# A fused attention and feed-forward kernel: ScalarE's function table loaded by a small exponential at the start, and another list that sets the order of all work

## The chip, the cores and the metric

The kernel runs on one core of one Trainium2 chip. The time is device microseconds of one execution. Three executions of the kernel before took 293.28 to 294.3 us, median 293.74.

## The reference

Sliding-window attention with a linear bias by distance, over 8 batches, 8 heads, 576 positions and a head size of 64, and then a feed-forward layer with a squared relu; in short:

```python
scores = scale * np.matmul(q, k.transpose(0, 1, 3, 2))
rel = pos[:, None] - pos[None, :]
bias = slopes[:, None, None] * (-np.abs(rel).astype(np.float32))[None, :, :]
mask = (rel >= 0) & (rel < window)                 # window = 128
scores = np.where(mask, scores + bias[None], -1000000000.0)
attn = softmax(scores)
x = np.matmul(attn, v)                             # to 4608 tokens of 512
h = x @ w_in                                       # 512 -> 2048
g = np.maximum(h, 0.0) ** 2
out = g @ w_out                                    # 2048 -> 512
```

Inputs and output are float32; the kernel computes in bfloat16 with float32 accumulation.

## The kernel before

The positions are cut into blocks of up to 128, numbered m = 0 to 35. The first block of each of the 8 batches (0 to 7) has no block before it; blocks 8 and up see the block before them too. For each block the work is: load q and k (`lkq`) and v (`lv`), transpose q and k (by TensorE with copies out, `tp` and `ev`, for blocks 0 to 7; by DMA transposes on SyncE's queue, `kqT`, after that), scores (`s`), exponentials on ScalarE (`e`), masks on VectorE (`m`), the product with v (`pv`), its normalisation on VectorE (`r`, `n`), and a transpose of the result (`xp` and `x`; `x` alone, by DMA, from block 8 on). Blocks 0 to 3 take their bias into PSUM by two matmuls of `ident` with `slopes` (`b`, line 774) ahead of the scores; the others are multiplied by `masks`, exponentials of the distance.

Block 0 is special: SyncE and ScalarE issue the loads of its k and q as float32 (`lk0`, `lq0`, line 523), VectorE casts them (`ck0`, `cq0`), and TensorE transposes k (`tp0.0`, line 610) and q (`tp0.1`). All other loads stand in GpSimd's queue: q and k, v, the weights w_in in five pieces (`w_in`), w_out in four (`w_out`). A first load waits in the queue behind nothing but GpSimd's own work, such as the `iota` that gives the distances; `ident` and `dist` (lines 423, 429, 430) are made from it by VectorE, and `slopes` from `dist` by VectorE and ScalarE.

Tokens are worked in 9 groups g of 512. The up phase (512 -> 2048) of groups 0 to 2 is direct (`u`, units of 8 or 16 matmuls); groups 3 to 8 use Strassen-like products with sums of weights (`us`) and of tokens (`ut`): `f`, in seven products, with sums and copies on VectorE and ScalarE. Relu and square (`relu`, `sq`) follow on ScalarE or VectorE. The down phase (2048 -> 512) is direct for group 0 (`o`, quarters of an output tile) and Strassen-like for the rest (`p`, seven products of two halves, `S1` to `S4` sums of g on VectorE, `ws` weight differences).

What sets the order: a list of about 1,680 task names, `ORDER`, written out in the kernel. Each name's instructions are emitted in that order; a trailing `+` picks the second of a task's possible engines, `:n` its PSUM banks. Every engine executes its own instructions in the emitted order, with semaphore waits between engines. The planner's durations (`BEGIN`, `S_PE`, the numbers in `plan.add`) pick nothing any more, except one thing: where the plan sees a gap ahead of a TensorE task in the first 30 us, `fill` (line 376) emits stand-in matmuls of zeros into that task's bank, one for each 56 ns of 0.85 of the gap. Eight larger stand-ins run at the very start (`warm`, line 574).

Of the kernel before, what the change touches and what calls it, by code (L numbers as in the profile page):

```python
# [36 lines left out]
S_PE = 360.0  # L37
# [16 lines left out]
    lk0.0 lk0.1 lkq1 warm0 one0.1 warm:6 one0.0 lq0.0 lq0.1 iota lkq2 ident dist1 slope0.3+ slope0.1+ slope1.0  # L54
    slope1.2 slope1.1 slope1.3+ slope0.2 ck0 lv0 slope0.0 b0:36 tp0.0:2 ev0.0.2 lv1 ev0.0.0+ cq0 w_in0 one0.7 one0.3
    one0.4 lv2 tp0.1:2 ev0.1.0 ev0.1.2 tp1.0:4 tp1.1:7 ev1.0.0+ w_in1 ev1.0.2+ s0 ev1.1.2+ ev1.1.0 e0.0 b1:50 e0.1
    one0.2 one0.5 one0.6 tp2.0:7 lkq3 tp2.1:1 s1 ev2.0.2+ ev2.0.0 ev2.1.2+ ev2.1.0 e1.0 pv0.0:6 pv0.1:3 r0.0 b2:17
    r0.1 n0.0 w_in4 s2 e1.1 n0.1 pv1.0:4 lv3 e2.0 pv1.1:5 r1.0 b3:36 n1.0 e2.1 xp0.0:2 r1.1 lkq4 n1.1 x0.0 pv2.0:0
    pv2.1:1 r2.0 xp1.0:7 n2.0 u0.0.0:2 x1.0 r2.1 n2.1 reluu0.0.0 lkq5 mask1.4 xp2.0:5 mask1.0 squ0.0.0 u0.1.0:4 x2.0
    tp3.0:0 mask1.2 reluu0.1.0 u0.0.1:1 w_in2 ev3.0.0+ ev3.0.2 tp3.1:7 u0.3.0:0 reluu0.0.1 ev3.1.2 w_in3 ev3.1.0  # L60
    squ0.0.1+ s3 squ0.1.0 lv4 reluu0.3.0 dist0 e3.0 u0.2.5:2 e3.1 w_out0 pv3.0:1 r3.0 pv3.1:5 u0.2.4:6 r3.1
    reluu0.2.5 one1.2 tp4.0:7 one1.0 one1.1 n3.0 n3.1 reluu0.2.4 one1.7 one1.6 tp4.1:3 xp3.0:4 ev4.1.0 tp5.0:5 x3.0+
    tp5.1:2 u0.5.2:4 lv5 lkq6 ev5.0.0+ squ0.2.4 w_out1 u0.5.3:6 ev5.1.0 one1.5 mask1.3 squ0.3.0 ev4.0.0+ squ0.2.5+
# [20 lines left out]
    r11.0 s13 n11.0 x10 pv11.1:3 u2.0.0:0 e13.0 r11.1 n11.1 e13.1 u2.0.2:4 e13.2 e13.3 x11 m12.0 m12.1 u2.0.6:1
    reluu2.0.2 m13.0 u2.0.4:6 us3.3 reluu2.0.0 st1.2.1 squ2.0.0 u2.0.1:4 kqT16 reluu2.0.4 u2.0.5:3 squ2.0.2 st1.3.1
    m13.1 pv12.0:0 pv12.1:5 lkq18 reluu2.0.5 st1.3.0 u2.0.7:7 squ2.0.4 reluu2.0.6 st1.7.3 st1.7.2 r12.0 squ2.0.5
    reluu2.0.1 u2.0.3:2 n12.0 reluu2.0.7 lv16 r12.1 kqT17 n12.1 squ2.0.6 squ2.0.7+ squ2.0.1 pv13.0:3 lv15 pv13.1:1
    reluu2.0.3 r13.0 s14 n13.0 st1.4.2 lv17 r13.1 u2.1.2:0 n13.1 e14.0 squ2.0.3 x12 lv18 e14.1 u2.1.0:4 mc14
# [5 lines left out]
    p2.5.1 lv21 n15.0 r15.1 n15.1 m16.1 x15 s17 s2_2 p2.7.0 p2.7.1 e17.0 S4.2.0 e17.2 c11_2 e17.1 lkq20 s5_2+ p2.3.0
    c22_2 kqT19 kqT21 e17.3 pv16.0:0 r16.0 m17.1 s18 n16.0 p2.3.1 m17.0 e18.0 e18.2 c12_2 e18.3 p2.4.0 kqT23
    pv16.1:4 m18.1 e18.1 r16.1 m18.0 pv17.0:5 pv17.1:0 n16.1 st2.2.0 st2.3.0 p2.4.1 s3_2 pv18.0:6 f3.0.1:7 f3.1.1:4
    r17.0 n17.0 st2.7.2 r17.1 s1.3.0:3 f3.2.1:5 n17.1 st2.2.1 ut3.0 ut3.1 s1.3.1:1 r18.0 lkq22 s1.3.2+:2 f3.0.2 x16
    pv18.1:0 reluf3.0.2 f3.0.6 s2.3.0 f3.1.2 n18.0 f3.0.5 sqf3.0.2 lv22 reluf3.1.2 ut3.2 ut3.3 f3.3.1:6 r18.1 s5.3.0
    f3.0.7 n18.1 kqT20 lv20 sqf3.1.2+ f3.2.2 c22.3.0 f3.0.3 c12.3.0 f3.1.6 reluf3.2.2 sqf3.2.2+ lkq25 x18 f3.1.5
    s2.3.1 f3.2.6 f3.0.4 reluc12.3.0 sqc12.3.0 f3.1.7 lkq26 s1.3.3+:3 s5.3.1 f3.1.3 st2.3.1 reluc22.3.0 sqc22.3.0+  # L100
    kqT22 reluf3.0.4 f3.3.2 reluf3.3.2 f3.2.5 c22.3.1 f3.1.4 c12.3.1 f3.3.6 s5.3.2 s2.3.2+ f3.2.7 sqf3.3.2+
    reluc22.3.1 sqf3.0.4 sqc22.3.1+ reluc12.3.1 f3.2.3 c22.3.2 c12.3.2 f3.3.5 p3.1.0:0 s2.3.3 st2.7.3 s5.3.3 x17
    f3.3.7 reluc22.3.2 reluc12.3.2 sqc12.3.2+ sqc22.3.2 sqc12.3.1 c22.3.3 reluc22.3.3 reluf3.1.4 f3.2.4 reluf3.2.4
# [5 lines left out]
    m22.1 p3.4.1 r21.0 s3_3 m22.0 pv21.1:5 kqT24 f4.0.1:7 s1.4.0:0 st3.7.3 f4.1.1:4 ut4.0 s1.4.1:3 n20.1 kqT26 n21.0
    ut4.1 pv22.0:2 lkq27 pv22.1:6 r22.1 f4.0.2 ut4.2 reluf4.0.2 f4.0.6 r22.0 n22.0 f4.1.2 ut4.3 n22.1 s2.4.0 r21.1  # L110
    f4.0.5 n21.1 s5.4.0 f4.0.7 lv23 f4.2.1:2 sqf4.0.2 lv24 f4.0.3 f4.1.6 reluf4.1.2 f4.1.5 sqf4.1.2+ c22.4.0 c12.4.0
    reluc12.4.0 s5.4.1+ s2.4.1 lv26 f4.0.4 reluc22.4.0 f4.1.7 s1.4.2:0 f4.2.2 reluf4.0.4 f4.1.3 sqc22.4.0+ sqc12.4.0
# [168 lines left out]
def kernel(  # L281
# [1175 lines left out]
```

## Time and profile before

| | |
|---|---|
| median of three executions | 293.74 us (293.28 to 294.3) |
| profiled execution, its own time | 294.23 us |
| span of the profiled execution, first to last instruction | 292.4 us |
| mean granted TensorE clock | 0.992 |
| busy: TensorE, VectorE, ScalarE, GpSimd | 281.1, 234.3, 207.3, 104.1 us |
| DMA packets, bytes | 159915, 39.68 MB |

The views used are: the page (busy time and share of each engine); the waits (engine and line that waited, what it waited for, us in total, times, longest); the stretches (busy time of each engine between two times, granted TensorE clock as a share of full speed, DMA share, GB/s); the timeline (start, length, engine, line, operation, output <- inputs, count, and in brackets the idle time before it and what ended it); the chain of waits that ended last (start, length, what); and a line's own view, which gives how long its DMAs took from issue to landing. PE is TensorE, PEld its weight loads, DVE is VectorE, ACT ScalarE, POOL GpSimd, SP SyncE; SPq and ACTq are DMA issues there. A matmul of 256 columns shows as 273 ns, since matmuls overlap; eight of them that follow each other advance 0.87 us.

### The profile page before, as it was taken

Reading aid. Unit: us, or ns where it says so; the run is one execution under the profiler, and the core shown is the slowest. Engines: PE = TensorE matmul, PEld = TensorE weight load, DVE = VectorE, ACT = ScalarE, POOL = GpSimd, SP = SyncE. Lnnn points to the kernel's source line nnn. Section 1 sums busy time; section 2 is a strip of 40 time slices with the busy share of each in tenths; the row PEclk is TensorE's granted clock in tenths of the full one; section 3 lists DMA queues with packets and bytes.
Section 4 is the critical chain, followed back from the end, with each engine's and each line's share of the span. In section 5 each row is a group of like instructions: output and inputs, shape, how many; then the busy total and the mean of one; then the engine's idle time right before and its main releaser. Section 6 shows DMA issues by size and latency. Waiting matters only on the chain.

```text
span 292.4 us, 9410 instructions
## 1 busy us (share of the span) xinstructions
PE 281.1 (96%) x3832; PEld 235.8 (81%) x3837; DVE 234.3 (80%) x570; ACT 207.3 (71%) x429; POOL 104.1 (36%) x132
## 2 busy tenths in 40 slices
PE   6799999999999999999899998999999999999994
PEld 2588745888889888887688887888888889888884
DVE  2545375968978698999799989999999998898933
ACT  3598933987847955887559964898868777777830
POOL 8965552709704744362427049550000000000000
PEclk9799999999999999999999999999999999999999
DMA  8999999999999999999999999999944112210123
GB/s 143 165 196 199 201 180 134 139 161 179 155 157 163 188 143 131 135 185 164 160 137 193 207 117 150 158 183 135 169 93 110 36 38 65 67 36 5 60 84 108
DMA packets 159915, 39.68 MB, mean 136 GB/s; under 512 B 142336, under 2 KB 159360, under 8 KB 159872
## 3 DMA queue, kind: packets, MB, share of 16 engines
q0 software_dynamic: 104432, 18.10, 86.7%
q1 hardware_dynamic: 54640, 20.33, 44.0%
q10 hardware_dynamic: 800, 0.66, 0.8%
q8 instruction: 30, 0.49, 0.7%
q14 instruction: 13, 0.11, 0.2%
HBM read 36.70 MB, written 9.44 MB: 158 GB/s over the span
## 4 chain that ended last, share of the span: by engine, by line
PE 86%; DVE 9%; ACT 2%; issue 1%; POOL 1%; DVEq 0%; POOLq 0%; ACTq 0%
PE o L1249 28%; PE h L1079 23%; PE h L977 15%; PE pv L830 6%; PE o L1160 5%; PE s L680 4%; DVE P L728 2%; PE tp L607 2%; DVE g L1384 1%; DVE rt L1104 1%; DVE sums L1384 1%; PE xp L874 1%; DVE g L948 1%; PE s L774 1%; PE o L1341 1%
## 5 line engine op out<-in xcount | busy, mean ns | idle before, releaser
L1249 PEld LDWEIGHTS <-g 128*128 128x128 bf16 x624 | 59.5, 98 | 9.2 <-issue 1.1
L1249 PE MATMUL o<-w_out_sb,g 128*128 128x256 bf16 x512 | 63.0, 273 | 1.4 <-DVE g L1384 0.9
L933 ACT ACTIVATE rt<-h 128x512 bf16<-128x512 f32 (+1 forms) x97 | 55.9, 596 | 11.3 <-PE h L1079 5.6
L545 POOL DMA_DIRECT2D kq<-in_k_dram x32 | 27.2, 855 | 69.5 <-DMA kqT<-kq 67.2
L715 ACT ACTIVATE E<-s 128x384 bf16<-128x384 f32 x96 | 41.3, 498 | 10.7 <-PE s L680 10.5
L977 PE MATMUL h<-xT,w_in_sb 128*128 128x256 bf16 (+1 forms) x432 | 44.8, 261 | 0.0
L948 DVE TENSOR_TENSOR g<-rt 128x512 bf16<-128x512 bf16 (+1 forms) x90 | 35.6, 415 | 9.5 <-ACT rt L933 8.9
L977 PEld LDWEIGHTS <-w_in_sb 128*128 128x128 bf16 x432 | 37.7, 98 | 4.2
L1079 PE MATMUL h<-xT,w_in_sb 128*128 128x256 bf16 x288 | 40.2, 273 | 0.2 <-DVE vf L400 0.2
L1079 PEld LDWEIGHTS <-w_in_sb 128*128 128x128 bf16 x384 | 36.4, 98 | 4.9 <-issue 0.4
L946 ACT ACTIVATE g<-rt 128x512 bf16<-128x512 bf16 (+1 forms) x55 | 34.2, 631 | 1.3 <-DVE rt L1112 0.7
L728 DVE TENSOR_TENSOR P<-E,masks 128x1024 bf16<-128x1024 bf16 x48 | 32.1, 679 | 3.3 <-ACT E L715 2.9
L402 ACT ACTIVATE osb<-o 128x512 f32<-128x512 f32 x30 | 18.0, 599 | 22.9 <-PE o L1249 19.0
L1249 PE MATMUL o<-wsum,sums 128*128 128x256 bf16 x256 | 30.6, 273 | 0.1
L854 DVE TENSOR_TENSOR x<-pv,rec 128x256 bf16<-128x256 f32 x72 | 29.1, 417 | 1.1
L551 POOL DMA_DIRECT2D vt<-in_v_dram x32 | 27.0, 865 | 8.1 <-PE pv L830 3.4
L545 POOL DMA_DIRECT2D kq<-in_q_dram x32 | 27.3, 854 | 6.6 <-DMA w_out_sb<-in_moe_w_out_dram 2.6
L1079 PE MATMUL h<-ut,kqf 128*128 128x256 bf16 x192 | 27.5, 273 | 0.0
L1249 PEld LDWEIGHTS <-sums 128*128 128x128 bf16 x256 | 24.3, 98 | 3.6 <-DVE sums L1384 0.4
L830 PEld LDWEIGHTS <-P 128*128 128x128 bf16 x512 | 21.9, 98 | 3.3 <-DVE P L728 1.1
L1104 DVE TENSOR_TENSOR rt<-h,vf 128x512 bf16<-128x512 f32 x32 | 21.7, 682 | 2.1 <-ACT vf L402 0.9
L830 PE MATMUL pv<-vt,P 128*128 128x65 bf16 x384 | 20.5, 193 | 0.1
(100 smaller groups left out, 432.2 us busy)
## 6 DMA issues: line engine op xcount, KB each, us to landing
out_dram<-osb SPq DMA_DIRECT2D x53, 128.0 KB, 4.0
kq<-in_k_dram POOLq DMA_DIRECT2D x31, 128.0 KB, 6.6
kq<-in_q_dram POOLq DMA_DIRECT2D x31, 128.0 KB, 7.3
vt<-in_v_dram POOLq DMA_DIRECT2D x24, 128.0 KB, 6.8
w_out_sb<-in_moe_w_out_dram POOLq DMA_DIRECT2D x4, 512.0 KB, 12.7
w_in_sb<-in_moe_w_in_dram POOLq DMA_DIRECT2D x3, 512.0 KB, 9.8
vf<-in_v_dram POOLq DMA_DIRECT2D x8, 128.0 KB, 7.7
out_dram<-osb SPq DMA_DIRECT2D x4, 256.0 KB, 4.2
```

Source lines behind the costliest of these rows:

```text
L545: nc.gpsimd.dma_start(view(kq[s_kq[m].idx], i)[rows], from_)
L551: nc.gpsimd.dma_start(tile_of(s_v[m])[rows, :, 0:D], from_)
L715: nc.scalar.activation(o, s, AF.Exp, bias=0.0, scale=scale)
L728: nc.vector.tensor_tensor(Pt[sP.idx][:, g], strips(sE)[:, g], masks[:, g], op=ALU.mult)
L830: nc.tensor.matmul(sv.tile[:, hi * (D + 1):(hi + 1) * (D + 1)], prob, tile_of(s_v[mk])[:, h, 0:D + 1], start=mk == parts[0][2], stop=mk == m)
L854: nc.vector.tensor_tensor(o, heads(sv)[:, :, 0:D], sr.tile.unsqueeze(2).to_broadcast([n, 4, D]), op=ALU.mult)
L933: nc.scalar.activation(srt.tile[:, 0:n], slot.tile[:, 0:n], AF.Relu, bias=0.0, scale=1.0)
L946: nc.scalar.activation(o, i, AF.Square, bias=0.0, scale=1.0)
L948: nc.vector.tensor_tensor(o, i, i, op=ALU.mult)
L977: nc.tensor.matmul(slot.tile[:, f * w:(f + 1) * w], w_in_sb[:, cc, fc * 128:(fc + 1) * 128], xT[:, cc, lo % (XR * 128):lo % (XR * 128) + w ...
L1079: nc.tensor.matmul(slot.tile[:, j * 256:j * 256 + 256], a, b_, start=fresh and j == 0 and c == 0, stop=c == 1, skip_group_check=True)
L1249: nc.tensor.matmul(slot.tile[:, z * 256:z * 256 + 256], stationary(c), moving(c), start=fresh and z == 0 and c == 0, stop=c == F - 1, skip ...
```

## The change

One task is new, an exponential of one column that writes a place of `masks` which is written again later; it is placed behind ScalarE's second DMA issue. The list `ORDER` is replaced as a whole. Five planner durations change, which move the stand-in matmuls only: 29 small ones before, 41 now.

```diff
-S_PE = 360.0
+S_PE = 270.0
...
-    lk0.0 lk0.1 lkq1 warm0 one0.1 warm:6 one0.0 lq0.0 lq0.1 iota lkq2 ident dist1 slope0.3+ slope0.1+ slope1.0
+    lk0.0 iota one0.1 lk0.1 warm0 lkq1 warm:1 lq0.0 lq0.1 ident dist1 table slope0.1+ slope1.1 lv0 slope0.3+
...
-    BEGIN = {"POOL": 840.0, "SP": 740.0, "ACTQ": 740.0, "ACT": 3400.0, "DVE": 860.0, "PE": 1190.0}
+    BEGIN = {"POOL": 840.0, "SP": 740.0, "ACTQ": 740.0, "ACT": 2100.0, "DVE": 860.0, "PE": 1190.0}
...
-            t_mask[part].append(plan.add({"ACT": act(128)}, mkey + 1 + p, build_mask, [t_dist[part]], name=f"mask{part}.{p}", later=14000.0))
+            t_mask[part].append(plan.add({"ACT": act(128) + 42.0}, mkey + 1 + p, build_mask, [t_dist[part]], name=f"mask{part}.{p}", later=14000.0))
...
+    t_lq, = [t for t in plan.tasks if t.name == "lq0.1"]
+    plan.add({"ACT": 1480.0}, EARLY, lambda: nc.scalar.activation(masks[:, 0, 0, 0:1], warm[:, 0:1], AF.Exp, bias=0.0, scale=1.0),
+             [t_wz], name="table", after=t_lq)
...
-            t_tp[i] = plan.add({"PE": 4 * mm(128) + (123.0 if by_runs else 0.0)}, due - 60 + i, tp,
+            t_tp[i] = plan.add({"PE": 4 * mm(128) + (98.0 if by_runs else -25.0)}, due - 60 + i, tp,
...
-            t = plan.add({"PE": 213.0 + (449.0 if diag else S_PE)}, due - 32, scores,
+            t = plan.add({"PE": 213.0 + (340.0 if diag else S_PE)}, due - 32, scores,
...
-        ts = plan.add({"DVE": dve(n, 2), "ACT": act(n) + 58.0} if g >= SQ_G else {"DVE": dve(n, 2)}, key, run,
+        ts = plan.add({"DVE": dve(n, 2), "ACT": act(n) + 34.0} if g >= SQ_G else {"DVE": dve(n, 2)}, key, run,
...
-            tr = plan.add({"DVE": dve(512, 4), "ACT": act(512) + 58.0}, key, relu, [t], name=f"relu{name}.{g}.{u}")
+            tr = plan.add({"DVE": dve(512, 4), "ACT": act(512) + 34.0}, key, relu, [t], name=f"relu{name}.{g}.{u}")
```

How the list moves instructions, at the places that the prediction speaks of. First TensorE at the start, before, from the end of the stand-ins of the first biases (`s` is the PSUM tile of block 0's scores, `kq` block 0's cast k and q; the bracket names what a row waits for):

```order
L376 MATMUL s_143<-sums 128x128
L774 LDWEIGHTS ident [waits DVE_49]
L774 MATMUL s_143<-sums,ident 128x512 [waits Activation_49]
L774 LDWEIGHTS ident [waits DVE_49]
L774 MATMUL s_144<-sums,ident 128x512 [waits PE_49]
L610 LDWEIGHTS kq_73 [waits DVE_49]
```

And now, from the last of the eight larger stand-ins and the last of block 0's k transposes on:

```order
L574 MATMUL wm<-sums 128x512
L614 LDWEIGHTS kq_72 [waits DVE_49]
L614 MATMUL tp<-ident,kq_72 128x128
...
L778 LDWEIGHTS ident
L778 MATMUL s_155<-sums,ident 128x512
L778 LDWEIGHTS ident
L778 MATMUL s_156<-sums,ident 128x512 [waits Activation_49]
L376 LDWEIGHTS sums
```

The transposes of block 0's k now stand ahead of the biases, and sixteen stand-ins stand between the biases and the transposes of q.

ScalarE at the start, before (line 456 makes slopes, 402 copies transposed blocks out of PSUM):

```order
L523 DMA wsum<-in_k_dram 128x1x256
L523 DMA wsum<-in_q_dram 128x1x256
L456 ACT_TABLE_LOAD [waits DVE_49]
L456 ACTIVATE sums<-sums 128x128 [waits Pool_49]
L456 ACTIVATE sums<-sums 128x128 x4
```

And now:

```order
L523 DMA wsum<-in_k_dram 128x1x256
L523 DMA wsum<-in_q_dram 128x1x256
L579 ACT_TABLE_LOAD
L579 ACTIVATE masks<-sums 128x1 [waits DVE_49]
L456 ACTIVATE sums<-sums 128x128 [waits DVE_49,Pool_49]
L456 ACTIVATE sums<-sums 128x128 x2
```

The table load no longer waits for the distances, and ScalarE makes three slopes instead of five; VectorE makes the other five.

GpSimd's queue, before, from the load of block 3 on (`kq` in turn are blocks 3, 4 and 5; the 512-wide pieces of w_in are the last three):

```order
L542 DMA kq_74<-in_k_dram 128x2x256
L542 DMA kq_74<-in_q_dram 128x2x256
L483 DMA w_in_sb<-in_moe_w_in_dram 128x4x512
L551 DMA vf<-in_v_dram 128x8x64
L542 DMA kq_71<-in_k_dram 128x2x256
L542 DMA kq_71<-in_q_dram 128x2x256
L542 DMA kq_72<-in_k_dram 128x2x256
L542 DMA kq_72<-in_q_dram 128x2x256
L483 DMA w_in_sb<-in_moe_w_in_dram 128x4x512 x2
L551 DMA vf<-in_v_dram 128x8x64
L486 DMA w_out_sb<-in_moe_w_out_dram 128x4x512
```

And now, from the same place (blocks 3, 5 and 4):

```order
L542 DMA kq_74<-in_k_dram 128x2x256
L542 DMA kq_74<-in_q_dram 128x2x256
L483 DMA w_in_sb<-in_moe_w_in_dram 128x4x256
L551 DMA vf<-in_v_dram 128x8x64 x2
L483 DMA w_in_sb<-in_moe_w_in_dram 128x4x512 x3
L542 DMA kq_71<-in_k_dram 128x2x256
L542 DMA kq_71<-in_q_dram 128x2x256
L542 DMA kq_72<-in_k_dram 128x2x256
L542 DMA kq_72<-in_q_dram 128x2x256
L486 DMA w_out_sb<-in_moe_w_out_dram 128x4x512 x3
```

All of w_in stands ahead of blocks 4 and 5. Further up in the same queue the iota has moved from behind the first load to ahead of it.

Elsewhere the list keeps its build. Counted over the list, six squares of the `f` products go from VectorE to ScalarE and three relus of sums from ScalarE to VectorE; of every other kind of task at most two change engines. Between the first product of group 1 and that of group 2, VectorE's part of the list has in addition four weight sums (`us`), a weight difference (`ws`), an evacuation (`x7`), a copy (`s3_1`), a square, and two normalisations (`n6.1`, `n7.1`), which stood earlier, or with ScalarE, before. The DMA transpose ahead of scores 18 (`kqT18`) now stands ahead of two transposes of x, one load and five stores that stood ahead of it.

More of the change, by code (lines that the diff above doesn't have):

```diff
@@ L59 @@
[L59 to L63, printed above, removed]
@@ L84 @@
[L84 to L88, printed above, removed]
@@ L94 @@
[L94 to L103, printed above, removed]
@@ L109 @@
[L109 to L112, printed above, removed]
-    f4.2.6 c22.4.1 f4.1.4 sqf4.0.4 c12.4.1 lkq30 reluf4.2.2 f4.2.5 reluc22.4.1+ s2.4.2+ kqT27 reluf4.1.4 sqc22.4.1
@@ L134 @@
-    e30.2 p5.7.0 st4.3.0 e30.3 f6.0.5 m29.0 s5.6.0 f6.0.7 kqT34 s31 m29.1 f6.0.3 c22.6.0 p5.7.1 sqf6.0.2+ e31.0
-    m30.1 st4.4.2 reluc22.6.0+ kqT35 c12.6.0 e31.3 f6.0.4 e31.2 m30.0 pv29.0:4 p5.5.0:2 reluf6.0.4 m31.1 e31.1
-    st4.4.3 p5.5.1 reluc12.6.0+ r29.0 sqc22.6.0 x28 sqf6.0.4 s1.6.1:0 sqc12.6.0 pv29.1:5 pv30.0:6 n29.0 f6.1.2 r29.1
-    m31.0 pv30.1:7 f6.1.6 s5_5 reluf6.1.2 s2.6.1 r30.1 n29.1 r30.0 sqf6.1.2 p5.3.0 f6.1.5 n30.0 c22_5 n30.1 pv31.0:5
-    st5.7.2 s5.6.1 p5.3.1 r31.0 n31.0 x29 f6.1.7 c12_5 x30 f6.1.3 c22.6.1 s32 p5.4.0 e32.0 c12.6.1 e32.1 reluc22.6.1
@@ new lines @@
+    pv9.0:5 lkq15 p1.2.0 p1.2.1 r9.0 n9.0 squ1.1.1+ s10 c11_1 e10.0 pv9.1:3 e10.3 e10.1 e10.2 squ1.1.0 S1.1.0
+    p1.5.0:0 lv11 lv12 S2.1.0 lkq16 st1.2.0 r9.1 S4.1.0 x8 p1.5.1 s11 e11.0 p1.6.0 p1.6.1 n9.1 lv13 lkq17 s5_1
+    p1.3.0 x9 m10.0 m10.1 st0.2.0 e11.1 e11.3 e11.2 s2_1 lv14 s12 e12.0 kqT15 S3.1.0 pv10.0:3 p1.7.0 m11.0 us0.1
+    m11.1 e12.2 p1.7.1 e12.3 us3.1 e12.1 p1.3.1 c22_1 m12.1 s13 c12_1 kqT14 e13.0 pv10.1:2 r10.1 p1.4.0 e13.3 r10.0
+    m12.0 e13.1 n10.0 n10.1 e13.2 p1.4.1 pv11.0:6 pv11.1:0 pv12.0:3 x10 r11.0 n11.0 r11.1 n11.1 x11 pv12.1:4 r12.1
@@ new lines @@
+    reluu2.1.2 st1.7.2 st1.7.3 u2.1.1:2 reluu2.1.5 ml14 u2.1.6:4 squ2.1.2+ mf14 st1.3.0 m14.0 u2.1.4:1 reluu2.1.1
+    reluu2.1.6 x12 squ2.1.5+ reluu2.1.4 squ2.1.1 x13 us0.2 pv14.0:3 r14.0 squ2.1.6 st1.4.2 s15 squ2.1.4 p2.1.0:2
+    S1.2.0 e15.0 e15.3 p2.1.1 e15.1 e15.2 S2.2.0 pv14.1:0 m15.1 m15.0 s1_2:1 s16 e16.0 e16.1 n14.0 r14.1 e16.2
+    p2.2.0 p2.2.1 c11_2+ p2.6.0 pv15.0:6 lkq23 n14.1 r15.0 p2.6.1 n15.0 pv15.1:0 lv19 us3.2 e16.3 x14 lv21 s17 r15.1
+    n15.1 x15 S3.2.0 e17.0 e17.3 S4.2.0 s2_2 e17.1 m16.0 e17.2 lkq20 p2.5.0:3 p2.5.1 p2.7.0 st2.2.1 p2.7.1 pv16.0:0
@@ new lines @@
+    s5.3.1 st2.3.0 f3.1.7 f3.1.3 sqc22.3.0 sqc12.3.0 st2.7.2 s1.3.3:1 reluf3.0.4 lkq25 st2.3.1 n17.1 c22.3.1 f3.2.6
+    c12.3.1 x17 reluc22.3.1 f3.3.2 f3.3.6 f3.1.4 s2.3.2+ s5.3.2 reluf3.3.2 sqf3.0.4+ sqf3.3.2+ reluc12.3.1 f3.2.3
+    x16 f3.2.7 lkq24 sqc22.3.1 c12.3.2 f3.3.5 sqc12.3.1+ c22.3.2 kqT22 lkq26 p3.1.0:3 s2.3.3 s5.3.3 reluc12.3.2
+    f3.3.7 reluc22.3.2 sqc12.3.2 f3.2.4 reluf3.1.4 sqf3.1.4+ sqc22.3.2 reluf3.2.4 c22.3.3 pv18.1:2 r18.1 reluc22.3.3
+    sqc22.3.3+ n18.1 x18 f3.3.3 c12.3.3 f3.3.4 reluf3.3.4 p3.1.1 sqf3.2.4 reluc12.3.3 s19 s1_3:1 sqf3.3.4 p3.2.0
@@ new lines @@
+    f6.0.3 c12.6.0 e31.0 e31.3 reluc12.6.0+ p5.7.1 f6.0.4 reluf6.0.4 m30.1 m30.0 x28 reluc22.6.0 p5.5.0:2 e31.1
+    p5.5.1 s1.6.1+:0 e31.2 m31.1 pv29.0:7 pv29.1:4 pv30.0:5 m31.0 s5_5 pv30.1:6 r29.0 r30.0 n29.0 sqf6.0.2+
+    sqc22.6.0+ f6.1.2 reluf6.1.2 sqf6.0.4+ r30.1 f6.1.6 p5.3.0 c22_5 sqf6.1.2+ pv31.0:7 n30.0 p5.3.1 n30.1 f6.1.5
+    r31.0 r29.1 x30 s2.6.1 sqc12.6.0+ n29.1 s5.6.1 n31.0 c12_5 f6.1.7 s32 c22.6.1 pv31.1:2 e32.0 x29 p5.4.0 e32.2
+    r31.1 reluc22.6.1 e32.3 e32.1 st5.7.3 n31.1 p5.4.1 sqc22.6.1 m32.1 st5.3.0 f6.1.4 m32.0 s3_5 x31 f6.1.3
@@ new lines @@
+    n34.0 p6.7.0 sqf7.1.2+ mf35 r34.1 p6.7.1 m35.1 n34.1 pv35.0:4 f7.1.5 s1.7.3:2 c22_6 x34 pv35.1:5 s5.7.1 r35.0
+    n35.0 f7.3.2 f7.1.7 r35.1 n35.1 f7.1.3 x35 c22.7.1 p6.4.0 f7.3.6 reluf7.3.2 f7.3.5 c12.7.1 reluc12.7.1 sqf7.3.2
+    st6.2.1 st6.3.0 f7.2.1:5 sqc12.7.1 s5.7.3 p6.4.1 st6.7.2 s1.7.2+:3 st6.3.1 reluc22.7.1+ s3_6 s2.7.3+ sqc22.7.1
+    f7.3.3 f7.2.2 reluf7.2.2 st6.7.3 f7.2.6 s2.7.2 c12.7.3 reluc12.7.3 f7.3.7 sqf7.2.2+ f7.1.4 c22.7.3 reluc22.7.3
+    st6.4.3 f7.2.5 f7.2.7 st6.4.2 sqc12.7.3+ s5.7.2+ c22.7.2 sqc22.7.3+ reluf7.1.4 p7.1.0:6 f7.3.4 f7.2.3
```

171 lines of the change are left out of this document (88 added, 83 removed).

## The prediction

> **What bounds the kernel now.** I read the page's share line first, then the waits of TensorE, then the stretches, then the timeline of the start.
>
> ```profile
> PE 281.1 (96%) x3832; PEld 235.8 (81%) x3837; DVE 234.3 (80%) x570; ACT 207.3 (71%) x429; POOL 104.1 (36%) x132
> PE s L774 <- ACT sums L456: 1.6, 1, 1.6
> PE tp L376 <- DVE kqf L400: 0.9, 1, 0.9
> PE o L1249 <- DVE g L1384: 0.9, 1, 0.9
> PE pv L830 <- DVE P L728: 0.5, 2, 0.4
> PE o L1249 <- ACT osb L402: 0.5, 1, 0.5
> PE s L774 <- ACT kqf L402: 0.4, 1, 0.4
> PE o L1249 <- DVE osb L1321: 0.3, 1, 0.3
> PE h L1079 <- DVE vf L400: 0.2, 1, 0.2
> PE s L680 <- ACT rt L933: 0.2, 1, 0.2
> ```
>
> TensorE is busy 96% and the change takes no matmul of the result away. Only its waiting can shrink, and the stand-in matmuls (L574, L376) that fill it. The span of 292.4 leaves 11.3 us idle. The rows say where: 1.6 + 1.2 + 0.9 + 0.4 = 4.1 us in the start, and 0.9 + 0.5 + 0.5 + 0.3 + 0.2 + 0.2 = 2.6 us in the body, nearly all behind VectorE or ScalarE. No row names a DMA.
>
> ```profile
> 4.66:8.08 3.42, 1.11 (x10) 0.63 (x9) 0.55 (x2) 2.17 (x7) 3.42 (x5) 1.00 1.53 180
> 8.08:11.49 3.41, 2.90 (x34) 2.15 (x34) 1.79 (x11) 1.04 (x4) 3.41 (x5) 0.50 1.68 147
> 116.00:150.00 34.00, 32.38 (x469) 27.18 (x466) 31.34 (x75) 22.84 (x47) 12.41 (x15) 1.00 1.92 160
> 150.00:165.00 15.00, 15.00 (x202) 12.77 (x200) 14.70 (x38) 14.40 (x30) 7.89 (x9) 1.00 1.83 181
> ```
>
> These stretches give stretch and length, then busy time of PE, PEld, DVE, ACT, POOL, then granted clock, DMA share and GB/s. From 4.66 to 8.08 TensorE works 1.11 of 3.42 us, and the next stretch is granted half the clock. From 116 to 150 VectorE is busy 31.34 of 34 us and TensorE idle 1.62, more than half of the body's 2.6.
>
> ```profile
> 4.06 1.28 ACT L456 ACT_TABLE_LOAD   x1 [4.06 <-DVE sums L430]
> 5.35 1.11 ACT L456 ACTIVATE sums<-sums 128x128 bf16<-128x128 f32 x5
> 6.51 0.59 PE L774 MATMUL s<-sums,ident 128*128 128x512 bf16 x2 [1.55 <-ACT sums L456]
> 6.94 0.39 PE L610 MATMUL tp<-ident,kq 128*128 128x128 bf16 x4
> 8.12 0.42 DVE L400 CAST kq<-wsum 128x512 bf16<-128x512 f32 x1
> 8.74 0.63 PE L610 MATMUL tp<-ident,kq 128*128 128x128 bf16 x4
> L523 SPq DMA_DIRECT2D wsum<-in_q_dram x1: 825/825/825, 1.5 to 1.5; - x1
> DMA to landing us min/median/max: 4.4/4.4/4.4
> ```
>
> ScalarE waits for VectorE, loads its table (1.28), makes five slopes (to 6.46); only then run the biases of block 0, and behind them in TensorE's order (6.94) the transposes of k. VectorE copies them out and only then casts q, at 8.12, although q landed at 1.5 + 4.4 = 5.9.
>
> **The change part by part.** *Table and first transposes.* The small exponential waits only for a memset that is done near 1.2 us, and stands behind ScalarE's second DMA issue (near 2.0). Load 1.28 and the exponential (one column wide; above 0 and no longer than a slope's 1.11 / 5 = 0.22) end by 3.5, while ScalarE has nothing else; its three slopes of 0.22 follow by 4.2. Uncovered this would cost 1.5. The iota now runs ahead of the first GpSimd load, so VectorE has ident, distances and its five slopes behind it when k lands. The transposes of k then run at about 4.8 and no longer behind the biases, q is cast at 5.9 instead of 8.12: up to 2.2 us earlier. Sixteen stand-ins (0.50 / 9 = 0.056 each by the chain row below, 0.9 together) now stand ahead of q's transposes and hold 0.4 or so of this back; the 12 more stand-ins in all (41 for 29) are 0.7, in places where a landing is awaited.
>
> *What the start is worth.* The next limit is the loads. The set that was complete with the last third of w_in is complete in the new order with k and q of block 4 (blocks 4 and 5 moved behind w_in, order of POOL).
>
> ```profile
> L483 POOL DMA_DIRECT2D w_in_sb<-in_moe_w_in_dram x2: 750/761/772, 15.5 to 16.3; - x2
> DMA to landing us min/median/max: 9.8/10.7/11.6
> 16.64 0.50 PE xp L376 x9
> 17.36 0.89 PE h L977 x16
> 23.47 0.57 PE tp L607 x16
> 24.93 9.78 PE h L977 x112
> 34.70 0.55 PE s L680 x16
> 35.63 4.05 PE o L1160 x18
> 39.80 0.86 PE o L1160 x4
> 57.11 0.87 PE h L977 x8
> ```
>
> The two issues land at 15.5 + 9.8 = 25.3 and 16.3 + 11.6 = 27.9: one piece takes 2.6. I take the same 27.9 for the end of the same set. Afterwards TensorE then ends block 4's transposes at 27.9 + 0.57 / 2 = 28.2 and has left of group 0's up phase: transposes of block 5 (0.57), one unit of 16 matmuls (0.89), scores 4 (0.55), one quarter of an output (0.86), four units of 8 (4 x 0.87 = 3.48): 6.35, to 34.55. Before, the 112 matmuls end at 34.70, scores follow, and the same quarter ends at 35.63 + 0.86 = 36.49. That is 1.94 earlier. From it go 0.3, as that quarter needs the first w_out, which lands a piece later (27.9 + 2.6 = 30.5) and is wanted at 28.2 + 0.57 + 0.89 + 0.55 = 30.2; and 0 to 0.4 because all GpSimd loads start behind the iota. I take **-1.5** (bounds -2.2, the whole step of q's cast, and 0, if the loads lose what the start wins). The half clock from 8.08 I count at 0: TensorE will probably be busier in the stretch ahead, but what it does then waits for landings; at most half of the 2.90 busy microseconds, 1.4, could come of it.
>
> The Trainium skill ("DMA: Bandwidth & Descriptors", Anatomy of one DMA, SWDGE path) fits a GpSimd DMA at about 2.0 us plus its bytes over 436 GB/s. The trace disagrees: 11.6 us for one issue, since it stands behind others; by the fit alone no load would hold the start and it would bring 2.2.
>
> *The body.* Six squares go from VectorE to ScalarE, three relus the other way.
>
> ```profile
> L948 DVE TENSOR_TENSOR g<-rt 128x512 bf16<-128x512 bf16 (+1 forms) x90 | 35.6, 415 | 9.5 <-ACT rt L933 8.9
> L946 ACT ACTIVATE g<-rt 128x512 bf16<-128x512 bf16 (+1 forms) x55 | 34.2, 631 | 1.3 <-DVE rt L1112 0.7
> L1112 DVE TENSOR_SCALAR rt<-rt 128x512 bf16<-128x512 bf16 x36 | 10.7, 301 | 0.4
> ```
>
> VectorE loses 6 x 0.415 - 3 x 0.301 = 1.6 us. Of the 2.6 us of body waits 0.9 + 0.5 + 0.3 + 0.2 = 1.9 are VectorE's. The order around them is much the same (product 7 of group 4 still stands behind the same sums and masks), so I count a third: **-0.6**. Bounds: -2.6, all body waits gone, and +1.0, one new wait as long as the longest there.
>
> Sum: -1.5 - 0.6 = **-2.1**. The profiled execution took 294.23 us, 1.8 around its span of 292.4 and 0.5 above the median; the differences carry over, so 293.74 - 2.1 = **291.6 us**.
>
> **The rivals.** *The start's gain is lost at a landing.* TensorE has little room ahead of group 3:
>
> ```profile
> L861 SPq DMA_TRANSPOSE xT<-x x1: 1519/1519/1519, 109.6 to 109.6; - x1
> DMA to landing us min/median/max: 7.7/7.7/7.7
> 117.69 1.92 PE L1079 MATMUL h<-xT,w_in_sb 128*128 128x256 bf16 x16
> ```
>
> The last transposed x of group 3 lands at 109.6 + 7.7 = 117.3, its first product starts at 117.69: 0.4 spare. If the DMA queues are full to there, the landing cannot move and 0.4 is all that remains: 293.3. For it: the DMA share of 1.5 to 1.9 in all the stretches above. Against: this transpose is issued when VectorE has normalised the block, so it moves with TensorE, and the new order issues it earlier against TensorE's work; the one ahead of scores 18 now passes two others, a load and five stores.
>
> *VectorE becomes the bound earlier: slower.* Between the first product of group 1 and that of group 2 the new order gives VectorE four weight sums, a weight difference, an evacuation, a copy, a square and two normalisations more, near ten instructions of 0.4 to 0.7: about 4.9.
>
> ```profile
> 60.00:105.00 45.00, 45.00 (x732) 39.40 (x731) 34.86 (x82) 33.14 (x70) 23.53 (x29) 1.00 1.77 166
> ```
>
> There VectorE is busy 34.86 of 45 us; with 4.9 more, 39.8, 88%, near the 92% of the stretch with the waits. If it cannot use its idle time, as work comes in bursts, TensorE stalls there for about 3 of the 4.9: 293.74 - 1.5 + 3.0 = 295.2. It decides once more than 2.4 us of stall appear. Against: 150 to 165 is 98% full without a stall.
>
> *The loads don't hold the start.* If they land early enough, 2.2 remain of the start, and of the body waits half (1.3) go: 290.2. For it: the first stretches move fewer GB/s (147) than later ones, so the queue has room. (This is what the fit quoted from the skill would give.)
>
> *The change does not do what it says:* the table is loaded again or the small exponential is held up, and the rest cancels: 293.7. Against: one table load stands in the new order.
>
> **How the numbers follow.** Forecast 291.6 with 0.45, its own range 290.6 to 292.7; gain lost at the landing (293.3) 0.20; VectorE bound (295.2) 0.16; loads hold nothing (290.2) 0.14; nothing done (293.7) 0.05. The range 289.9 to 294.6 leaves out most of the slow case and the best end of the fast one. A measurement tells 0.3%, 0.9 us: below 292.9 is faster, above 294.6 slower. Faster: 0.43 + 0.14 = 0.57; the same: 0.20 + 0.05 + 0.02 = 0.27; slower: 0.16.
>
> **What would show it.** Start: the table load near 2 us, the first transposes near 4.8 and ahead of the biases, q's cast near 5.9; the first quarter of an output ending near 34.6 instead of 36.5, with waits for w_in or for block 4 on the way. Body: the same waits by name, fewer microseconds. Wrong would be: q's cast still near 8; a first quarter of an output near 36.5; a wait on DMA landings at group 3; a VectorE row above 1 us between 60 and 105.

## The result and the profile after

The changed kernel takes 290.5 us (median of 4 runs, 290.09 to 290.93) where the kernel before takes 293.84 us in the same job (4 runs, 293.28 to 294.3). The ratio is 0.9887, with a 95% interval of 0.9862 to 0.9913: about 3.3 us less. The profiled execution took 290.13 us with a span of 288.2 (before: 294.23 and 292.4). Lines of the new file are 4 higher from the exponential (L579) on.

The page's share line and all the waits of TensorE that the trace of the changed kernel lists (waiting engine and line, releaser, us in total, times, longest):

```profile
PE 280.9 (97%) x3844; PEld 237.0 (82%) x3849; DVE 234.7 (81%) x570; ACT 207.5 (72%) x430; POOL 104.3 (36%) x132
PE wm L574 <- DVE sums L420: 1.2, 1, 1.2
PE s L788 <- DVE kqf L400: 0.5, 1, 0.5
PE xp L376 <- DVE x L858: 0.4, 1, 0.4
PE s L778 <- ACT kqf L402: 0.3, 1, 0.3
PE o L1253 <- ACT o L402: 0.2, 1, 0.2
PE pv L834 <- DVE P L732: 0.2, 1, 0.2
PE s L778 <- issue: 0.2, 1, 0.2
```

TensorE's busy time is the same (280.9 for 281.1), so the whole gain is idle time in the sense of the page: 292.4 - 281.1 = 11.3 us before, 288.2 - 280.9 = 7.3 now. The 1.6 of the first biases and the 0.9 of the sums of g are gone. Of the body's 2.6 us of named waits two rows of 0.2 are left (o for o, pv for P). No row names a DMA.

The stretches that answer to those shown of before (stretch, length, busy us and instructions of PE, PEld, DVE, ACT, POOL, granted clock, DMA share, GB/s):

```profile
4.66:8.08 3.42, 3.34 (x33) 2.48 (x31) 1.35 (x8) 0.52 (x2) 3.42 (x6) 1.00 1.81 179
8.08:11.49 3.41, 2.71 (x48) 1.69 (x48) 1.10 (x4) 3.11 (x8) 2.69 (x4) 1.00 1.36 174
20.00:30.00 10.00, 10.00 (x147) 9.17 (x147) 3.69 (x14) 9.58 (x25) 5.43 (x7) 1.00 1.30 203
60.00:105.00 45.00, 44.91 (x760) 39.46 (x759) 36.48 (x87) 33.77 (x72) 24.41 (x30) 1.00 1.75 174
116.00:150.00 34.00, 33.67 (x488) 29.56 (x486) 32.16 (x81) 25.97 (x53) 14.89 (x18) 1.00 1.68 157
```

Read them against the rows in the prediction. From 4.66 to 8.08 TensorE is busy 3.34 us instead of 1.11, and the next stretch keeps the full clock. From 20 to 30, where the prediction has TensorE waiting for w_in, it is busy all the time. It was so in the kernel before too, a row that the prediction does not look at:

```profile
20.00:30.00 10.00, 10.00 (x150) 8.79 (x148) 3.88 (x17) 8.99 (x24) 6.53 (x9) 1.00 1.44 198
```

VectorE is busier from 60 to 105 (36.48 for 34.86), and TensorE stands still there for 0.09 us. From 116 to 150 TensorE's idle time has fallen from 1.62 to 0.33 although VectorE is busier than before.

The start in the timeline (start, length, engine, line, what, and in brackets the idle time ahead):

```profile
2.06 1.28 ACT L579 ACT_TABLE_LOAD   x1 [2.06 <-issue]
4.61 0.63 PE L614 MATMUL tp<-ident,kq 128*128 128x128 bf16 x4
5.04 1.06 PE L778 MATMUL s<-sums,ident 128*128 128x512 bf16 x2
6.18 1.50 PE L376 MATMUL tp<-sums 128*128 128x128 bf16 x16
6.37 0.68 DVE L400 CAST kq<-wsum 128x512 bf16<-128x512 f32 x1 [0.66 <-DMA wsum<-in_q_dram]
7.52 0.39 PE L614 MATMUL tp<-ident,kq 128*128 128x128 bf16 x4
```

The table is loaded at 2.06, k's transposes run ahead of the biases, and q is cast at 6.37 instead of 8.12 as soon as it has landed. The 16 stand-ins end at 6.18 + 1.50 = 7.68, and q's transposes overlap their end. In most of this TensorE runs at half its rate, although the granted clock of the stretch reads 1.00: four transposes take 0.63 us at 4.61, as in the half stretch of the kernel before, and 0.39 at 7.52.

Where the gain lies can be read by splitting the span at three score bursts (scores 6, 18 and 28), which both lists have in the same order. First the kernel before, then the changed one; columns as above:

```profile
4.60:50.53 45.93, 42.50 (x505) 29.83 (x509) 22.78 (x77) 31.49 (x77) 27.98 (x36) 0.96 1.66 180
113.27:187.10 73.83, 70.98 (x1055) 60.35 (x1052) 68.76 (x165) 53.50 (x110) 33.15 (x41) 1.00 1.85 162
```

```profile
4.60:49.96 45.36, 43.68 (x518) 30.48 (x521) 21.79 (x71) 30.40 (x72) 26.77 (x35) 1.00 1.66 182
111.91:183.23 71.32, 70.86 (x1068) 61.81 (x1065) 68.39 (x165) 54.66 (x113) 30.73 (x37) 1.00 1.81 161
```

Scores 6 start at 49.96 instead of 50.53: the start is worth 0.57 us in these two executions. (Three other profiles of the old start, in the runs below, have scores 6 at 51.52 to 51.60, so one profile sizes this badly.) Scores 18 to 28 are 2.51 us shorter, although the new list has 13 matmuls more between them, and TensorE's idle time there falls from 73.83 - 70.98 = 2.85 to 0.46. This is what the experiments had to confirm, since the prediction had it the other way round.

### The profile page after: what moved, and what is told of

It reads as the page before. It is cut to its first block, busy times and chain, and to the rows that moved or that the text cites. A ratio compares the mean times of both kernels' runs of the same rounds, so it can differ in the third digit from the quotient of the medians.

```text
span 288.2 us, 9417 instructions
## 1 busy us (share of the span) xinstructions
PE 280.9 (97%) x3844; PEld 237.0 (82%) x3849; DVE 234.7 (81%) x570; ACT 207.5 (72%) x430; POOL 104.3 (36%) x132
## 4 chain that ended last, share of the span: by engine, by line
PE 92%; DVE 3%; ACT 2%; issue 1%; ACTq 0%; DVEq 0%
PE o L1253 32%; PE h L1083 25%; PE h L981 14%; PE pv L834 6%; PE o L1164 5%; PE s L684 5%; PE wm L574 1%; PE tp L611 1%; DVE P L732 1%; PE xp L878 1%; ACT P L797 1%; PE o L1345 1%; ACT kqf L402 1%; DVE kqf L400 1%; PE tp L376 1%
## 5 line engine op out<-in xcount | busy, mean ns | idle before, releaser
L937 ACT ACTIVATE rt<-h 128x512 bf16<-128x512 f32 (+1 forms) x97 | 56.5, 597 | 11.2 <-PE h L981 7.9
L1083 PE MATMUL h<-xT,w_in_sb 128*128 128x256 bf16 x288 | 40.8, 273 | 0.0
L952 DVE TENSOR_TENSOR g<-rt 128x512 bf16<-128x512 bf16 (+1 forms) x84 | 32.8, 413 | 8.3 <-ACT rt L937 8.0
L950 ACT ACTIVATE g<-rt 128x512 bf16<-128x512 bf16 (+1 forms) x61 | 37.4, 632 | 1.0 <-DVE rt L1116 0.4
L402 ACT ACTIVATE osb<-o 128x512 f32<-128x512 f32 x33 | 19.8, 600 | 15.5 <-PE o L1253 11.3
L834 PEld LDWEIGHTS <-P 128*128 128x128 bf16 x512 | 22.7, 98 | 2.7 <-DVE P L732 0.5
L834 PE MATMUL pv<-vt,P 128*128 128x65 bf16 x384 | 21.1, 193 | 0.1
```

Source lines behind the costliest of these rows:

```text
L834: nc.tensor.matmul(sv.tile[:, hi * (D + 1):(hi + 1) * (D + 1)], prob, tile_of(s_v[mk])[:, h, 0:D + 1], start=mk == parts[0][2], stop=mk == m)
L937: nc.scalar.activation(srt.tile[:, 0:n], slot.tile[:, 0:n], AF.Relu, bias=0.0, scale=1.0)
L950: nc.scalar.activation(o, i, AF.Square, bias=0.0, scale=1.0)
L952: nc.vector.tensor_tensor(o, i, i, op=ALU.mult)
L1083: nc.tensor.matmul(slot.tile[:, j * 256:j * 256 + 256], a, b_, start=fresh and j == 0 and c == 0, stop=c == 1, skip_group_check=True)
```

## The experiments

Each ratio is against runs of the kernel before in the same job (medians 293.81 to 294.32), in brackets its 95% interval.

**The new start with the old body, and the reverse.** The list is cut at scores 6; behind the cut stand the tasks that are still missing, in the other list's order.

```diff
 ORDER = new[: "s6"] + [t for t in old if t not in new[: "s6"]]     # x1
 ORDER = old[: "s6"] + [t for t in new if t not in old[: "s6"]]     # x2
```

> The new list up to scores 6 (about 50 us, the end of group 0's down phase), with the early exponential and the new planner durations; behind that the old list. Theory A (from the two traces: about 1 us is gained at the start, the rest behind 50 us): 292.8 us, 0.9 to 1.3 below the kernel before, and the body waits of the kernel before (o for g, o for osb, pv for P, together near 2 us) come back. Theory B (the prediction's own split, the start 1.5 and more, the body 0.6): 291.1, two thirds of the gain or more are there already. Theory C (all is won at the start, and the body only inherits it): 290.5.

> The reverse: the old list up to scores 6, without the early exponential and with the old planner durations; behind that the new list. Theory A: 291.5 us, 2.3 below the kernel before, with the old waits of the start (s for sums 1.6, tp for kqf 0.9) and hardly a wait behind 50 us. Theory B: 293.2, 0.6 below. Theory C: 293.8, no difference.

x1: 0.9981 [0.9960, 1.0002], median 293.61, about 0.6 us below, with an interval that reaches no difference. x2: 0.9900 [0.9877, 0.9922], median 291.47, 2.9 below. The two add up to 3.5 and the whole change to 3.3. Theory A comes nearest, though x1 brought less than its 0.9 to 1.3. In x1 two of the three body waits that it names are back (o for osb is not):

```profile
PE o L1254 <- DVE g L1389: 0.9, 1, 0.9
PE pv L835 <- DVE P L733: 0.5, 2, 0.4
```

In x2 the start's waits stand as before, and the stretch between scores 18 and 28 is that of the changed kernel (71.00 us, 0.27 idle):

```profile
PE s L776 <- ACT sums L458: 1.4, 1, 1.4
PE tp L378 <- DVE kqf L402: 0.9, 1, 0.9
113.54:184.54 71.00, 70.73 (x1067) 61.57 (x1065) 68.26 (x165) 54.51 (x113) 30.56 (x38) 1.00 1.77 164
```

**How the body's gain is spread.** The cut of x1, but at scores 18.

> The new list up to scores 18 (near 112 us), behind that the old one. Theory A (by the traces TensorE's time beyond its matmuls is the same for both lists between scores 6 and scores 18, and 3.2 us differ behind that): the start's gain alone, 0.3 to 0.9 below the kernel before, 293.2, with the wait of o for g back. Rival (the gain of the body is spread evenly, a third of it lies ahead of scores 18): 292.2.

0.9976 [0.9955, 0.9996], 293.26 us: 0.7 below, with the wait of o for g at 0.9 again. So the gain of the body lies behind scores 18, as theory A has it.

**The largest body wait alone.** One task is moved in the old list.

```diff
-p4.3.0 pv24.1:4 m26.1 S3.4.0 p4.3.1
+p4.3.0 S3.4.0 pv24.1:4 m26.1 p4.3.1
```

> The old list with one edit: the third sum of g of group 4 (S3.4.0) stands on VectorE ahead of the mask product of block 26, which waits for TensorE's product with v of block 24. Theory A (that place on VectorE is the cause of the largest body wait, o for g 0.87 us): the wait goes and the time falls by 0.8 to 1.2, to 292.6 to 293.0. Rival (the wait moves to the next product with v for P, or to the first products of group 5, since VectorE has the same work there): 293.4 to 293.8.

0.9967 [0.9948, 0.9987], 292.91 us, 1.0 below. The timeline of the kernel before around that sum (ScalarE, VectorE, TensorE), and that of VectorE and TensorE with the edit:

```profile
171.15 0.48 ACT L715 ACTIVATE E<-s 128x384 bf16<-128x384 f32 x1
174.17 0.69 DVE L728 TENSOR_TENSOR P<-E,masks 128x1024 bf16<-128x1024 bf16 x1 [1.26 <-ACT E L715]
174.78 1.22 DVE L1384 TENSOR_TENSOR g<-g 128x2048 bf16<-128x2048 bf16 x1
173.65 0.41 PE L830 MATMUL pv<-vt,P 128*128 128x65 bf16 x8
176.05 1.92 PE L1249 MATMUL o<-w_out_sb,g 128*128 128x256 bf16 x16 [0.87 <-DVE g L1384]
```

```profile
172.09 1.29 DVE L729 TENSOR_TENSOR P<-E,masks 128x1024 bf16<-128x1024 bf16 x2
173.29 1.22 DVE L1385 TENSOR_TENSOR g<-g 128x2048 bf16<-128x2048 bf16 x1
174.63 0.69 DVE L729 TENSOR_TENSOR P<-E,masks 128x1024 bf16<-128x1024 bf16 x1
175.48 1.91 PE L1250 MATMUL o<-w_out_sb,g 128*128 128x256 bf16 x16
```

In the first, VectorE stands idle for 1.26 us ahead of the mask product of block 26, with the sum of g that product 7 needs queued behind it. The row names ScalarE's exponential, but that block's last exponential had ended at 171.15 + 0.48 = 171.63. What ended at 174.06 (173.65 + 0.41) is TensorE's product with v of block 24, which reads the P buffer that the mask product writes. So TensorE waited for VectorE, which waited for TensorE. With the sum ahead of the mask the circle is open: product 7 waits for nothing, and the idle time between scores 18 and 28 is 1.55 us instead of 2.85.

**What of it rests on the P buffer.** In the changed list the same mask product stands ahead of block 24's product with v, and so does not wait for it; the expectation tells which heads that touches, in both lists. Here it waits again:

```diff
 for m in (12, 26, 27, 31): "m<m>.1" is moved to directly behind "pv<m-2>.1"
```

> In the changed kernel's list the mask product of the second four heads of blocks 12, 26, 27 and 31 stands ahead of the product with v of the block two before, which reads the same one of the two P buffers; there the older block's four heads are multiplied by the younger block's probabilities (the old list does the same in blocks 27 and 31). Here these four mask products stand behind that product with v. Theory A (the body's gain comes from the sums of g standing ahead of the masks on VectorE, not from the wait for the P buffer that is missing): within 0.5 us of the changed kernel, 290.3 to 291.0. Rival (TensorE's wait of 0.87 us at product 7 of group 4 went because VectorE no longer waits for the P buffer): it comes back, 291.2 to 291.6, with a row o for g of 0.5 or more.

0.9872 [0.9848, 0.9896], 290.29 us: the time of theory A. But its premise is not what the changed kernel does. There, too, the sum of g stands behind the mask product of block 26, the last of the three mask products in the first row; it runs without a wait, ahead of the product with v of block 24 that still has to read the buffer:

```profile
168.58 1.89 DVE L732 TENSOR_TENSOR P<-E,masks 128x1024 bf16<-128x1024 bf16 x3
170.39 1.22 DVE L1388 TENSOR_TENSOR g<-g 128x2048 bf16<-128x2048 bf16 x1
171.82 0.41 PE L834 MATMUL pv<-vt,P 128*128 128x65 bf16 x8
```

So in the changed kernel the 0.87 us went because a wait was left out, as the rival says. This also makes the result wrong there: the product with v uses another block's probabilities in four heads of blocks 10, 24, 25 and 29 (in the kernel before, of 25 and 29). y1 sets the mask product behind that product with v, and with it behind the sum. VectorE's timeline of y1 has both things, the wait for the buffer and the sum ahead of it:

```profile
169.68 1.29 DVE L733 TENSOR_TENSOR P<-E,masks 128x1024 bf16<-128x1024 bf16 x2
170.88 1.22 DVE L1389 TENSOR_TENSOR g<-g 128x2048 bf16<-128x2048 bf16 x1
173.44 1.29 DVE L733 TENSOR_TENSOR P<-E,masks 128x1024 bf16<-128x1024 bf16 x2 [1.25 <-PE pv L835]
```

Now the bracket names TensorE. The wait is as long as in the kernel before (1.25 for 1.26), and it costs nothing measurable, as no sum stands behind it: the same time can be had with the wait kept. The profiled execution (291.70 us) was the longest of the seven, with 1.61 us idle between scores 18 and 28 where the changed kernel had 0.46, for which the runs give no cause.

**Engines without places.** The old list with the new choice of engine for every task behind scores 6 (a "+" added or taken away in 90 names; most of them are swaps, and the six squares and three relus are what is left net).

> The old list, with the new list's choice of engine behind scores 6 for every task that has two (90 tasks differ; six squares more on ScalarE and three relus more on VectorE in all). Theory A (the body's gain lies in the places, not in the engines): between 293.2 and 294.3, the body waits stay near 2.6 us. Rival (the prediction's term: VectorE loses 1.6 us and a third of the waits behind it goes): 293.2, 0.6 below. Rival (the engines bring the whole of it): 291.5 or less.

1.0317 [1.0288, 1.0346], 302.93 us: 9.3 us slower, which no theory had. Two of the largest of its waits behind scores 6:

```profile
PE h L1080 <- DVE rt L1105: 1.5, 2, 0.9
PE s L681 <- ACT rt L934: 1.1, 1, 1.1
```

They stand in a list of thirteen, over nearly everything that the two engines pass to TensorE. The same engines cost 9.3 us in the old places, and are part of the 2.9 won in the new ones: the choice of engine by itself did not win them. Nor did VectorE's busy time fall: 234.3 us before, 234.7 in the changed kernel, 236.7 in this one.

**The early table load.** Taken out of the changed kernel, and put alone into the old one, behind `lq0.1`.

```diff
-    plan.add({"ACT": 1480.0}, EARLY, lambda: nc.scalar.activation(...), [t_wz], name="table", after=t_lq)   # x3
+    plan.add({"ACT": 1480.0}, EARLY, lambda: nc.scalar.activation(...), [t_wz], name="table", after=t_lq)   # z1
```

> The changed kernel without the small exponential: ScalarE then loads its table (1.28 us) ahead of its first slope, near 3.5 us, with the new order otherwise. Theory A (the load only delays the biases, which now stand behind the transposes of k and in front of those of q): the biases move from 5.04 to about 6.3, q's transposes lose 0.5 to 0.9, and the time is 0.3 to 0.8 above the changed kernel's, 290.8 to 291.3 us. Rival (the whole load is uncovered, the prediction's price for that case): 291.8 to 292.0. Rival (the load hides behind q's landing and the loads that follow): 290.5.

> The old list with the small exponential alone, behind ScalarE's second DMA issue. There the distances are ready only at 4.06 us, so the load (1.28 us) is taken out of the path: slopes end near 5.2 instead of 6.46, the biases start near 5.2, q is cast near 6.9 instead of 8.12. Theory A (the start is worth little at the end): 0.2 to 0.6 below the kernel before, 293.3. Rival (the start passes on in full): 1.2 below, 292.5. Rival (a transfer or the clock takes it back): 293.8.

x3: 0.9854 [0.9827, 0.9880], 289.82 us; the interval overlaps that of the changed kernel. Without the exponential the load starts all the same at 2.12:

```profile
2.12 1.28 ACT L458 ACT_TABLE_LOAD   x1 [2.12 <-DVE sums L432]
3.41 0.71 ACT L458 ACTIVATE sums<-sums 128x128 bf16<-128x128 f32 x3
```

The iota, now ahead of the loads, has the distances ready by then, so the load for the first slope itself starts only 0.06 us later than the load for the small exponential did (2.06). The expectation took the load to start near 3.5, the time of the first slope behind the exponential; that was the mistake. The iota's new place, which makes the difference here, was not run alone. z1: 0.9937 [0.9915, 0.9959], 292.43 us, 1.9 below: the first rival, and more. In the old list the distances come at 4.06, and there the load is on the path. The task also moves the planner's gap, and 13 stand-ins instead of 3 stand ahead of the biases, so the 1.9 us belong to the load and ten stand-ins together; no run has the load alone:

```profile
4.58 1.40 PE L377 MATMUL s<-sums 128*128 128x128 bf16 x13
8.32 0.40 PE L615 MATMUL tp<-ident,kq 128*128 128x128 bf16 x4 [0.32 <-DVE kq L401]
```

Scores 6 start at 49.38 there, earlier than in the changed kernel. Why x1, whose scores 6 start at 49.84, was 1.3 us slower in its median than z1, with nearly the same body, stays open: their profiled spans are 291.2 and 291.7.

**The first transposes.** In the changed list `b0:73` moves ahead of `tp0.0:2`.

> The changed kernel with the biases of block 0 ahead of the transposes of its k again. Biases start near 4.9 and take 0.6 to 1.1 us, k's transposes then near 5.9 instead of 4.6, q's cast near 7.4 instead of 6.4. Theory A (of a step of 1 us at q's cast less than half is left at the end): 0 to 0.5 above the changed kernel, 290.5 to 291.0. Rival (the step passes on): 291.5.

0.9870 [0.9842, 0.9898], 290.51 us, no difference from the changed kernel: which of the two comes first is not worth a measurable time. The step of 1 us at q's cast that the expectation starts from did not come: q is cast at 6.48 (6.37 in the changed kernel), only 10 stand-ins stand ahead of q's transposes, and these start at 7.58 (7.52). So the run does not say what such a step would leave at the end.

**Stand-ins and the clock.** The old start with more stand-ins, and the changed kernel with none (`FILL = 0.0`).

```diff
-for _ in range(int(task.gap * FILL / 56.0) if task.gap > 200.0 else 0):
+for _ in range({"b0": 17, "tp0.1": 16}.get(task.name, int(task.gap * FILL / 56.0)) if task.gap > 200.0 else 0):   # x4
```

> The kernel before with more stand-in matmuls: 17 for 3 ahead of the first biases, 16 for 5 ahead of q's transposes, so that TensorE is busy between 4.66 and 8.08 and the clock of the next stretch is not halved. Theory A (as predicted, the half clock between 8.08 and 11.49 costs nothing, as the work there waits for copies): 293.8 us, no difference. Rival (the half clock costs up to half of its 2.90 busy us): 292.4 to 293.2. If the granted clock still drops, the run says nothing on either.

> The changed kernel without its 41 small stand-in matmuls. Theory A (16 of them stand ahead of q's transposes and take 1.05 to 1.50 us in 0.95 us of waiting, so they hold the start back by 0.1 to 0.5, and the clock costs little): q's transposes at 7.1 instead of 7.5, the time 0 to 0.5 below the changed kernel's, 290.0 to 290.5. Rival (without them TensorE is idle for 1 us between 4.6 and 8, the clock is halved in the stretch behind, as in the kernel before): 0.5 to 1.4 above, 291.0 to 291.9.

x4: 0.9981 [0.9963, 1.0000], 293.33 us, 0.6 below, with an interval that just reaches no difference. The clock did not drop in it, so keeping it up is worth some half a microsecond: between "no difference" and the rival. That is net of the 25 added stand-ins, with which q's transposes start at 9.15 instead of 8.74. x8: 0.9938 [0.9914, 0.9962], 291.81 us, 1.3 above the changed kernel. The size is the rival's, but the mechanism is not seen: its granted clock shows no half, q's transposes run at 7.08, as theory A has it, at the full rate, and its scores 6 start at 49.51, no later than with stand-ins (49.54 in x3, 49.96 in the changed kernel). The loss lies far behind the stand-ins, in two gaps for which the trace names only the issue. First q's transposes, then the two gaps:

```profile
7.08 0.40 PE L616 MATMUL tp<-ident,kq 128*128 128x128 bf16 x4 [1.16 <-DVE kq L402]
PE pv L836 <- issue: 0.8, 1, 0.8
PE o L1255 <- issue: 0.7, 1, 0.7
```

The gaps stand near 113 and 141 us. Why 41 matmuls less in the first 30 us bring gaps there was not found out, and what the stand-ins are worth in the new list stays open.

**Both that cost nothing, together.** x3's and y1's edits.

> The changed kernel without the small exponential, and with the mask products of blocks 12, 26, 27 and 31 behind the product with v of the block two before. Theory A (neither costs anything): 289.8 to 290.6, a ratio near 0.987. Rival (the two together cost what each of them hid): 291.2 or more.

0.9849 [0.9821, 0.9877], 289.82 us (289.44 to 290.27): with x3 the lowest median, though not by more than its interval. It is also the version to keep, since its mask products wait for the P buffer at those four places.

## Why the prediction was right in its sign and time, and wrong in its parts

The sign came out, and the time nearly (291.6 predicted, 290.5 measured, just below the forecast's own range of 290.6 to 292.7). But the sum of -1.5 and -0.6 was made of two mis-sized terms whose errors went opposite ways; that the sum came near is luck.

*The start, -1.5: over-sized.* It measured 0.6 and 0.7 in the timed runs of x1 and x5, and 0.57 at scores 6 in the two profiles. The steps were right as far as q's cast (6.37, predicted 5.9). The step that failed is "The next limit is the loads". TensorE is busy 10.00 of 10.00 us from 20 to 30, before and now, and it has no wait for w_in or block 4. The chain of waits of the changed kernel shows the sequence that the prediction laid behind a landing at 27.9 running instead behind TensorE's own work:

```profile
22.09 6.15 PE h L981 x72
28.24 1.01 PE tp L611 x32
...
31.94 3.49 PE h L981 x32
```

The same work ends at 31.94 + 3.49 = 35.43, not at 34.55; before it was 36.49. That is 1.06 of the 1.94, and by scores 6 0.57 is left; what took the rest is not shown. The transposes of q came 1.2 us earlier (7.52 for 8.74) and not 2.2. The stand-ins held them back by 0.44 (7.08 in x8), which the prediction put at 0.4; it missed that q's cast would start at 6.37, behind q's landing, and not at 5.9, and take 0.68 us instead of 0.42.

*The half clock, 0: nearly right.* x4 puts it at 0.6, of a bound of 1.4. The start is less steady than one profile shows. In x2 the same list began with TensorE at half its rate for longer, and so it did in x6 and y2. The same 16 transposes, before and in x2:

```profile
11.68 0.64 PE L607 MATMUL tp<-ident,kq 128*64 128x128 bf16 x16
```

```profile
12.42 1.06 PE L609 MATMUL tp<-ident,kq 128*64 128x128 bf16 x16
```

Scores 6 came at 51.60 there, 1.07 later than in the kernel before's profile, at 51.60 in x6 and at 51.52 in y2. Against these three the new start is about 1.6 earlier at scores 6, so the profile on which the prediction rests is the early one of four.

*The body, -0.6: far too small.* x2 measured 2.9, a little beyond the bound of 2.6. The step that failed is "product 7 of group 4 still stands behind the same sums and masks ... so I count a third". What it says of the order is true, but it compared which tasks stand ahead, and not which of them wait. One mask product that waits for TensorE, ahead of one sum that TensorE needs, was the whole of the 0.87, and y2 gets 1.0 us by one move. The other 1.9 of the 2.9 was not taken apart: the remaining waits behind scores 18 went with the rest of the new order, and which moves did it is not shown. The other part of the term, VectorE's load, was the wrong lever. The squares and relus did move as it says (squares 35.6 us before and 32.8 now, these relus 10.7 and 11.6), but other work took their place: VectorE's busy time did not fall at all (234.7 for 234.3), and in x6 the same choice of engines costs 9.3 us.

*The rivals.* The gain was not lost ahead of group 3: its first product starts 0.83 us earlier (116.86 for 117.69), where the rival leaves 0.4. VectorE as a bound from 60 to 105 did not come, although VectorE did get more work there (1.62 us, of the 4.9 feared): no row of TensorE names it. "The loads don't hold the start" was right in its premise and came nearest in time (290.2), but for the opposite reason in its sum: less from the start than its 2.2, more from the body than its 1.3. With it falls the weight that the 11.6 us from issue to landing had: TensorE never waited for that landing. The fit of the Trainium skill ("DMA: Bandwidth & Descriptors", Anatomy of one DMA) had pointed at that premise, though its times do not agree: it starts from 2.0 us plus the bytes, and the shortest load of GpSimd's in the changed kernel's trace took 3.3 us from issue to landing, the five pieces of w_in 6.9 to 11.6. "The change does not do what it says" holds for the table alone: in the new order the early load is worth nothing, and the time comes from elsewhere.

## What to carry to other kernels

Before sizing a wait on an engine that works in order, ask what the instruction ahead of the late one waits for: a buffer that is read by the waiting engine itself makes a circle, and one move opens it. A landing bounds a stage only if the busy engine would be idle there; a stage that is 100% busy between two starts passes on its own work, not the transfer's time. What an edit is worth can hang on another: the early table load, with the stand-ins that came along with it, is worth 1.9 us where the distances come late, and the load is worth nothing where they come early, so each is to be tried with and without the other. And a wait that goes away may have been left out: where an instruction that overwrites a buffer moves ahead of its last reader in the list, the time gets shorter and the result wrong.

## What the runs showed of the hardware

The profiler's releaser of a wait on two engines can be the wrong one: the 1.26 us were put down to an exponential that had ended 2.5 us earlier, and with the order changed the same wait of 1.25 us was put down to TensorE.

A table load costs 1.28 us on ScalarE, and the next activation follows at once (2.12 + 1.28 = 3.40, the slope at 3.41).

TensorE's rate in the first 14 us is not the same in each execution of one start: the same 16 transposes took 0.64 us at 11.68 in one and 1.06 us at 12.42 in another. The granted clock does not tell this: it reads 1.00 in x2 from 0 to 14 us. With the stretch from 4.66 to 8.08 filled to 3.34 of 3.42 us, at half rate in the main, no drop was seen in the next one. The half stretch in the kernel before lasted 11.49 - 8.08 = 3.41 us. The Trainium skill ("TensorE: Matmul & The Clock Gate", Part 1: The HAM clock gate) has a window of 3413 ns that runs freely and doesn't start with the kernel; the length agrees, and a window that falls differently on the same idle time would explain why two executions of one start differ. The runs did not test that.
